# Attention and feed-forward on one core: the first batch's x split from PSUM, and the mask of 14 heads added by TensorE

## The chip, the core and the metric

The kernel runs on one core of one Trainium2 chip. The metric is the device time of one execution in microseconds: 943.42 us before, the median of three runs (942.66 to 944.47). A core has TensorE (PE, matmuls out of SBUF into PSUM), VectorE (DVE), ScalarE (ACT), GpSimd (POOL) and SyncE (SP), which here issues every DMA. Each engine works through its own instructions in order; they meet at semaphores.

## The reference, cut to what matters

Eight batches of eight heads; 512 local and 32 global tokens each; heads of 64. Then a feed-forward layer on all 8 x 544 = 4352 tokens of 512 features.

```python
s_g = scale * q_g @ k_all.T                  # global queries see all 544 keys
out_g = sm(s_g) @ v_all
s_ll = where(|i - j| <= 32, scale * q_l @ k_l.T, -1e9)
s_l = concat([scale * q_l @ k_g.T, s_ll])    # local queries: 32 global keys and a window
out_l = sm(s_l) @ v_all                      # sm: subtract the row's maximum, exp, divide by the sum
x = concat([out_g, out_l]).reshape(4352, 512)
h = x @ w_in                                 # 512 -> 2048
g = h * erf(softplus(h))
out = g @ w_out                              # 2048 -> 512
```

The weights come as 64-bit floats, which the kernel turns into 32-bit ones itself.

## The kernel before, in words

**Precision and matmuls.** Every feed-forward operand is split into a high part, rounded to TensorE's `float32r` type, and a low part, the remainder; a product is three matmuls (high by high, high by low, low by high). `h` of one unit (128 rows of the hidden layer by 512 tokens) is 12 matmuls of 512 columns.

**A pair of heads** (`attention`, line 369). Local queries are taken in 16 windows of 32; each sees an extent of 128 key columns. `scores` fills two PSUM banks `s` for the two heads with 64 small matmuls. Then, for each head: `mask_max` on VectorE adds the mask out of `cs` to each of four blocks of 128 x 128, writes the result to SBUF (`sm`) and takes the row's maximum (`mx`) with the same custom instruction, four per head; a subtraction of the maximum, on VectorE or GpSimd; one exponential on ScalarE over all 512 columns; four transposes on TensorE into a PSUM bank `t`; a copy to `pt`; 16 matmuls with the values (`o`, whose last column is the row's sum); the division (`rs`, `norm`) into `xn`, 128 tokens by 128 features in four blocks.

**From attention to the feed-forward part.** After each second head VectorE transposes `xn` in blocks of 32 x 32 into `xT` (line 474), and four DMAs store it to the DRAM scratch `xsc[b]`, feature rows by tokens, with the tokens of each row in a moved order. Later `load_x` (line 706) loads a batch's x back in two halves, `rx`, and splits each into `xh` (VectorE or ScalarE) and `xl` (GpSimd or VectorE), putting the tokens in order again. `attention_global` (line 502) treats the 32 global queries of four heads at a time; for the first batch it is put off until head 12.

**Two passes over the feed-forward part.** The hidden layer is worked in two halves. The first pass takes one batch after another: `load_x`, eight units of `h` (`unit`), the nonlinearity in groups of four units (`gate`: on ScalarE a table load, four softplus, a table load, four erf, a table load back to the exponential), and the projection `op` (`project`), whose partial result goes to DRAM. The second pass takes batches in pairs with a Strassen-like scheme (`pair_blocks`, `products`: matmuls `pa` to `pd`), and reads `xsc` again, that of the first batch too. A last unit, `h_g`, serves the global tokens.

**Weights.** `to_fp32` (line 614) loads a raw block (`raw`), takes its bits together on VectorE (three integer instructions and one that clears denormals, tile `top`), with one ScalarE instruction beside them; `split` makes the high and low parts. For the first pass four blocks `w_in` and four `w_out` of two halves each are converted during the first heads (keys `WIN`, `WOUT`); `keep_unit` converts the second half of `w_out` to DRAM; `convert_in` the second half of `w_in`, once attention is over.

**What sets the order.** Nothing is ordered by hand. `Program.add` (line 107) takes each operation with its estimated duration on each engine that may run it, a key (a due time in units of the feed-forward part) and the buffers that it reads and writes. `schedule` (line 144) replays the estimates in time: on each free engine it takes the ready operation with the smallest key, no further ahead of the oldest one left than `AHEAD`, if its buffers are free; an operation that two engines could do goes to the one that the estimates favour (`BIAS`). The result is the fixed order of instructions on each engine, SP's DMA queue included. So keys and estimates, not only the operations, decide what the chip runs next. Heads get keys by `HKEYS`: a list of head numbers and keys with straight lines between. While the estimated time is under `FILL` = 50, `filler` puts matmuls on constants (`spare`) where TensorE would be idle, so that its clock stays up.

**PSUM.** Eight banks: two for `h` (pool `h`), six for all else (pool `a`): scores, transposes, values, global attention, projections.

Of the kernel before, what the change touches and what calls it, by code (L numbers as in the profile page):

```python
# [11 lines left out]
F32 = mybir.dt.float32  # L12
# [37 lines left out]
LATER, GFIRST = 12, (-2.0, -1.7)  # L50
NORMAL = 1.125 * 2.0**-15
STRAIGHT = False
# [208 lines left out]
def kernel(  # L261
# [74 lines left out]
    load(HKEYS[0][1] - QLEAD + 0.001, CS, cst, 360)  # L336
    PG = fixed(attn.tile([P, NENT * WB], F32, name="pg"))
# [30 lines left out]

    def attention(b, h, key):
# [15 lines left out]

        if h % 2 == 0:
            st["s"] = SS = [psum_a([P, 4, P], f"s_{nm}_{i}") for i in range(2)]

            def scores():
                for t in range(4):  # L390
                    for i in range(2):
                        for a in range(4):
# [6 lines left out]
                                start=True,  # L399
                                stop=True,  # L400
                            )

            add({"PE": 1.24}, key, scores, [Q, K], SS, heat=2048)
# [4 lines left out]
        def mask_max():  # L408
            for t in range(4):
# [11 lines left out]
        add({"DVE": 0.9}, key, mask_max, [S, CS], [SM, MX])  # L421
        add({"DVE": 0.6, "POOL": 1.03},
            key,
            lambda e: vec[e].tensor_tensor(
                SM.ap, SM.ap, MX.ap.unsqueeze(2).to_broadcast([P, 4, P]), ALU.subtract
            ),
            [MX],
            [SM],
        )
        add({"ACT": 0.62}, key, lambda: act(SM.ap, SM.ap, AF.Exp, scale=scale), [TAB], [SM])  # L430
# [8 lines left out]
        add({"ACT": 0.6, "DVE": 0.6}, key + STEP * 2, lambda e: copy(e, PT.ap, T.ap), [T], [PT])  # L439
# [32 lines left out]
        add({"DVE": 0.335, "ACT": 1.28}, key + STEP * 3, norm, [O, RS], [XN])  # L472
        if h % 2 == 1:
            XT = abuf([P, 4, P], f"xT_{nm}", "xT", 1)
            add({"DVE": 0.62},
                key + STEP * 4,
                lambda: dve.transpose(
                    XT.ap.rearrange("p j (t d) -> p j t d", d=WB), XN.ap.rearrange("p t (j d) -> p j t d", d=WB)
                ),
                [XN],  # L480
                [XT],
            )
            rows = xsc[b][P * p : P * p + P, :].rearrange("(j d) (a x) -> a d j x", d=WB, a=4)

            def store():
                for a in range(4):
                    dma(rows[a], XT.ap[WB * a : WB * a + WB])

            add({"SP": 4 * SPT}, key + STEP * 4, store, [XT, ATTN], [XSC[b, p]], moved=262.0)
# [10 lines left out]
    held, NH, GTURN = [], H, fixed(None)  # L500

    def attention_global(b, j, VA, qk, key):
# [36 lines left out]
        add({"ACT": 0.98}, key, exps, [GA, GB, NM, TAB], [PG])  # L539
# [7 lines left out]
        for T, m0 in ((T1, 0), (T2, 3)):  # L547
            add({"PE": 0.33}, key + STEP * 2, lambda T=T, m0=m0: transposes(T, m0), [PG, CS], [T], heat=384)
            add(
                {"ACT": 0.5, "DVE": 0.46},  # L550
# [41 lines left out]
        add({"DVE": 0.22, "ACT": 0.62}, key + STEP * 3, spread, [O, HALF], [XG])  # L592
# [21 lines left out]
    def to_fp32(key, src, name, TOP, ABS, deps, lead=RLEAD):  # L614
# [7 lines left out]
        add({"ACT": 0.7}, key, lambda: act(ABS.ap(), word(1).bitcast(F32), AF.Abs), [RAW], [ABS.buf])  # L622
# [13 lines left out]
        add({"DVE": 1.55}, key, bits, [RAW], [TOP.buf])  # L636
        add({"DVE": 0.6}, key, normal, [ABS.buf], [TOP.buf])

    def split(key, TOP, HI, LO):
# [625 lines left out]
```

## Time and profile before

| | |
|---|---|
| median of three runs | 943.42 us |
| the profiled execution | 945.86 us |
| its span, first to last instruction | 944.1 us |
| busy: TensorE | 914.6 us (97%) |
| busy: VectorE | 643.0 us (68%) |
| busy: ScalarE | 536.0 us (57%) |
| busy: GpSimd | 401.8 us (43%) |
| DMA traffic | 173.26 MB, mean 184 GB/s |

Times in the profile are microseconds from the span's start unless marked ns. A row of a group reads: line, engine, operation, output<-inputs, shapes, count | busy us, mean ns of one | idle time of the engine just before, and what ended it. Nearly all instructions are recorded under a helper's line (L299 matmuls, L300 transposes, L301 ScalarE, L311 VectorE and GpSimd, L303 DMAs), so they are told apart by their tiles. A row of the timeline begins with its start and its length. Matmuls overlap in the pipeline: a record of 0.39 us can stand for a step of 0.23. SPq is the DMA queue's issuing.

### The profile page before, as it was taken

The numbers are of one execution on the slowest core, as the hardware profiler recorded it, in microseconds if no ns is written. First come the engines' busy times: TensorE is split into PE (matmuls) and PEld (weight loads), VectorE is DVE, ScalarE is ACT, GpSimd is POOL, SyncE is SP. The second block draws the span as 40 slices with busy tenths as digits, with TensorE's granted clock in tenths as the row PEclk, the third lists the DMA queues.
The fourth block names the chain that finished last, engine by engine and source line by source line (L and its number), as shares of the span: only waits on it lengthen the run. The fifth ranks groups of instructions, "written<-read, shape, count | busy, mean of one in ns | idle before, by whom it ended". The sixth has DMA issues, their size and how long they took to land.

```text
span 944.1 us, 22303 instructions
## 1 busy us (share of the span) xinstructions
PE 914.6 (97%) x8937; PEld 736.0 (78%) x8937; DVE 643.0 (68%) x1484; ACT 536.0 (57%) x895; POOL 401.8 (43%) x295
## 2 busy tenths in 40 slices
PE   8899889999999999999999999999999999999997
PEld 6667667777777877777888887888888888888886
DVE  5899799877788685674676959357656446544363
ACT  3547757535586565445766676527727544842590
POOL 1233456332353332132364668334737537541250
PEclk9999899999999999999999999999999999999999
DMA  9876776468677765542406063844642636253422
GB/s 347 278 238 213 231 230 225 138 208 284 209 247 227 238 200 161 163 142 58 157 33 257 34 257 112 310 192 178 234 155 91 239 110 226 81 193 134 157 90 67
DMA packets 89535, 173.26 MB, mean 184 GB/s; under 512 B 13272, under 2 KB 38872, under 8 KB 89432
## 3 DMA queue, kind: packets, MB, share of 16 engines
q1 hardware_dynamic: 89432, 171.84, 54.0%
q8 instruction: 70, 1.15, 0.5%
q14 instruction: 33, 0.27, 0.1%
HBM read 133.53 MB, written 38.27 MB: 182 GB/s over the span
## 4 chain that ended last, share of the span: by engine, by line
PE 79%; DVE 9%; issue 2%; DMA 1%; SPq 0%; ACT 0%; DVEq 0%
PE op L299 37%; PE h L299 16%; PE pc L299 4%; PE pd L299 4%; PE pa L299 4%; DVE top_out L311 3%; PE o L299 2%; PE s L299 2%; PE pb L299 2%; PE t L300 2%; PE h_g L299 1%; PE go L299 1%; PE ga L299 1%; DVE sm L311 1%; PE gt L300 1%
## 5 line engine op out<-in xcount | busy, mean ns | idle before, releaser
L299 PE MATMUL op<-wouth,gh 128*128 128x512 f32 x544 | 218.3, 401 | 0.0
L299 PE MATMUL op<-woutl,gh 128*128 128x512 f32 x544 | 213.2, 392 | 1.2 <-DVE woutl L311 1.2
L299 PE MATMUL op<-wouth,gl 128*128 128x512 f32 x544 | 213.0, 392 | 0.0
L311 POOL TENSOR_TENSOR gl<-sp,gh 128x512 fp32r<-128x512 f32 x66 | 92.7, 1409 | 111.7 <-ACT gh L301 70.0
L299 PEld LDWEIGHTS op<-wouth,gh 128*128 128x128 f32 x544 | 102.7, 189 | 23.3 <-issue 1.4
L299 PEld LDWEIGHTS op<-wouth,gl 128*128 128x128 f32 x544 | 102.7, 189 | 22.1
L302 ACT ACT_TABLE_LOAD x92 | 118.0, 1283 | 2.4 <-PEq L1252 0.7
L299 PEld LDWEIGHTS op<-woutl,gh 128*128 128x128 f32 x544 | 102.9, 189 | 20.9 <-DVE woutl L311 1.5
L301 ACT ACTIVATE gh<-sp 128x512 fp32r<-128x512 f32 x104 | 63.3, 629 | 95.4 <-PE op L299 66.2
L299 PE MATMUL h<-xh,winh 128*128 128x512 f32 (+1 forms) x288 | 113.8, 395 | 0.0
L299 PE MATMUL h<-xh,winl 128*128 128x512 f32 (+1 forms) x288 | 110.2, 383 | 0.0
L299 PE MATMUL h<-xl,winh 128*128 128x512 f32 (+1 forms) x288 | 110.1, 382 | 0.1
L311 POOL TENSOR_TENSOR sm<-sm,mx 128x512 f32<-128x512 f32 x43 | 49.0, 1149 | 131.9 <-DVE mx L311 77.3
L311 DVE TENSOR_TENSOR gl<-sp,gh 128x512 fp32r<-128x512 f32 x70 | 70.7, 1019 | 38.6 <-ACT gh L301 37.3
L311 POOL TENSOR_TENSOR sp<-sp,hs 128x512 f32<-128x512 f32 x46 | 68.3, 1505 | 55.0 <-ACT sp L301 55.0
L301 ACT ACTIVATE sp<-sp 128x512 f32<-128x512 f32 x136 | 75.0, 620 | 0.4
L311 DVE CUSTOM_DVE_ANT_0 sm<-s,cs 128x128 f32<-128x128 f32 x256 | 57.2, 283 | 21.2 <-PE s L299 12.5
L299 PEld LDWEIGHTS h<-xh,winh 128*128 128x128 f32 x288 | 55.0, 191 | 11.3 <-issue 1.4
L299 PEld LDWEIGHTS h<-xh,winl 128*128 128x128 f32 x288 | 54.8, 190 | 10.8
L299 PEld LDWEIGHTS h<-xl,winh 128*128 128x128 f32 x288 | 55.1, 191 | 9.9 <-issue 0.5
L301 ACT ACTIVATE sm<-sm 128x512 f32<-128x512 f32 x64 | 39.9, 631 | 40.5 <-POOL sm L311 35.7
L301 ACT ACTIVATE hs<-h 128x512 f32<-128x512 f32 x44 | 26.2, 595 | 62.0 <-PE h L299 62.0
(186 smaller groups left out, 1824.0 us busy)
## 6 DMA issues: line engine op xcount, KB each, us to landing
wq<-wq SPq DMA_DIRECT2D x28, 896.0 KB, 6.4
vb<-in_vB_dram SPq DMA_DIRECT2D x64, 325.0 KB, 4.0
rx<-xsc SPq DMA_DIRECT2D x32, 512.0 KB, 7.2
va<-in_vA_dram SPq DMA_DIRECT2D x64, 195.0 KB, 3.8
k<-in_kE_dram SPq DMA_DIRECT2D x32, 384.0 KB, 5.7
q<-in_qT_dram SPq DMA_DIRECT2D x32, 272.0 KB, 5.3
part<-os SPq DMA_DIRECT2D x34, 256.0 KB, 3.8
os<-part SPq DMA_DIRECT2D x34, 256.0 KB, 4.1
```

Source lines behind the costliest of these rows:

```text
L299: pe = lambda n, *a, **k: pinned(nc.tensor.matmul(n, *a, **k))
L300: tr = lambda *a, **k: pinned(nc.tensor.transpose(*a, **k))
L301: act = lambda *a, **k: pinned(nc.scalar.activation(*a, **k))
L302: table = lambda name: pinned(nc.scalar.preload_act_table_set(name))
L311: return lambda *a, **k: pinned(f(*a, **k))
```

## The change

It has four parts.

1. **`straight`.** For the first batch, each pair's `xn` is transposed by TensorE (four transposes into a PSUM bank `x`), one copy on ScalarE or VectorE rounds it into the high part, and VectorE subtracts that from the bank into the low part. `load_x(0, 0)` hands these tiles to the units and loads nothing. Since the second pass still wants `xsc[0]`, a third instruction copies the bank to `xT` with the tokens in the moved order, and one DMA stores it, both keyed 1.547 later.
2. **14 front heads** (`FRONT`). `csr` is a `float32r` copy of the mask and the identity. For the first seven pairs, one matmul of 512 columns (identity by mask) starts each score bank, and the 64 small matmuls add onto it. VectorE takes the maxima of all four blocks with one `tensor_reduce` out of PSUM and scales them by -1/8; ScalarE takes the exponential out of PSUM in four instructions with the maxima as bias, and no subtraction is left. The other 50 heads are as before.
3. **Keys.** `HKEYS`, `WIN`, `WOUT`, `KEEP`, `GATE1`, `PROJ1` and most other timing constants have new values.
4. **Estimates.** The durations that the planner assumes are changed in some 25 places (a ScalarE copy of 512 columns 0.58 to 0.52, say); the operations in those places are the same.

```diff
-HKEYS = ((0, -6.35), (8, -3.85), (22, 0.53), (64, 42.58))
-STEP, GKEY = 0.06, -0.15
-QLEAD, VLEAD, RLEAD, XLEAD = 0.755, 0.15, 0.011, 2.0
-GOFF, POFF = 1.27, 4.29
-WIN, WOUT = (-4.26, -3.26, -2.26, -1.26), (4.0, 5.0, 6.0, 7.0)
-KEEP, KSTEP, FIRST = 20.0, 2.5, (6.0, 9.0)
-CV0, CVS, CVO = (46.5, 54.5), 1.8, (71.0, 72.0, 73.0, 74.0)
-QLEAD2, XDEL = 4.0, 1.6
-GATE1, GATE2, PROJ1, PROJ2 = (11.0, 17.0), (20.0, 25.0), 15.0, 23.0
+HKEYS = ((0, -6.695), (8, -5.399), (22, 0.494), (64, 36.876))
+STEP, GKEY = 0.15, -0.654
+QLEAD, VLEAD, RLEAD, XLEAD = 1.111, -0.093, 0.011, 2.475
+GOFF, POFF = 0.46, 5.993
+WIN, WOUT = (-5.592, -4.592, -4.119, -2.592), (0.525, 1.379, 2.986, 3.986)
+FRONT = 14
+KEEP, KSTEP, FIRST = 15.253, 2.161, (8.718, 8.308)
+CV0, CVS, CVO = (44.889, 46.213), 1.64, (73.778, 71.216, 73.428, 75.096)
+QLEAD2, XDEL = 2.637, 2.359
+GATE1, GATE2, PROJ1, PROJ2 = (17.232, 16.792), (19.085, 26.545), 19.111, 19.37
-BIAS, AHEAD = 0.65, 10.4
+BIAS, AHEAD = 0.637, 14.185
-LATER, GFIRST = 12, (-2.0, -1.7)
+LATER, GFIRST = 12, (-3.159, -2.767)
-STRAIGHT = False
+STRAIGHT, XLATE = True, 1.547
...
+    csr = attn.tile([P, 512 + P], F32R, name="csr")
+    add({"ACT": 0.75}, HKEYS[0][1] - 0.01, lambda: copy("ACT", csr, cs[:, : 512 + P]), [CS], [CSR])
...
             def scores():
+                for S in SS if front else ():
+                    pe(S.ap.rearrange("p t k -> p (t k)"), csr[:, 512:], csr[:, :512], start=True, stop=True)
...
-                                start=True,
+                                start=not front,
...
-            add({"PE": 1.24}, key, scores, [Q, K], SS, heat=2048)
+            add({"PE": 1.24 + 0.5 * front}, key, scores, [Q, K, *[CSR] * front], SS, heat=2048)
...
+        def largest():
+            dve.tensor_reduce(MX.ap, S.ap, axis=AX.X, op=ALU.max)
+            dve.tensor_scalar(MX.ap, MX.ap, -scale, None, op0=ALU.mult)
+
+        def exps():
+            for t in range(4):
+                act(SM.ap[:, t, :], S.ap[:, t, :], AF.Exp, bias=MX.ap[:, t : t + 1], scale=scale)
+
+        if front:
+            add({"DVE": 0.8}, key, largest, [S], [MX])
+            add({"ACT": 1.05}, key, exps, [TAB, S, MX], [SM])
+        else:
...
+            if b == 0 and STRAIGHT:
+                straight(p, XN, key)
+            else:
...
+    def straight(p, XN, key):
+        i, j = divmod(p, 2)
+        if j == 0:
+            X0[i] = [mbuf([P, 2, SL], F32R, f"x{x}_0_0_{i}", f"x{x}", 3) for x in "hl"]
+        HI, LO = X0[i]
+        X = psum_a([P, SL], f"x_{p}")
+        def transposes():
+            for t in range(4):
+                tr(X.ap[:, P * t : P * t + P], XN.ap[:, t, :], ident)
+        add({"PE": 0.47}, key + STEP * 4, transposes, [XN, CS], [X], heat=512)
+        add({"ACT": 0.52, "DVE": 0.62}, key + STEP * 4, lambda e: copy(e, HI.ap[:, j, :], X.ap), [X], [HI])
+        add({"DVE": 0.62}, key + STEP * 4,
+            lambda: dve.tensor_tensor(LO.ap[:, j, :], X.ap, HI.ap[:, j, :].bitcast(F32), ALU.subtract), [X, HI], [LO])
...
+        add({"ACT": 0.55, "DVE": 0.69}, key + STEP * 4 + XLATE,
+            lambda e: copy(e, XT.ap.rearrange("p (a t q) -> p t a q", a=4, q=WB), moved(X.ap)), [X], [XT])
+        add({"SP": SPT}, key + STEP * 4 + XLATE, lambda: dma(xsc[0][P * p : P * p + P, :], XT.ap), [XT, ATTN], [XSC[0, p]], moved=262.0)
...
+        if c == 0 and STRAIGHT:
+            return [(*X0[i], j) for i in range(2) for j in range(2)]
```

More of the change, by code (lines that the diff above doesn't have):

```diff
@@ L438, in attention @@
         add({"PE": 0.47}, key + STEP * 2, transposes, [SM, CS], [T, PT], heat=512)
-        add({"ACT": 0.6, "DVE": 0.6}, key + STEP * 2, lambda e: copy(e, PT.ap, T.ap), [T], [PT])
+        add({"ACT": 0.52, "DVE": 0.61}, key + STEP * 2, lambda e: copy(e, PT.ap, T.ap), [T], [PT])
         O = psum_a([P, 4, D + 1], f"o_{nm}")
@@ L470, in norm, with store @@
                     act(XN.ap[:, t, r0 : r0 + D], O.ap[:, t, :D], AF.Copy, scale=RS.ap[:, t, :])
-        add({"DVE": 0.335, "ACT": 1.28}, key + STEP * 3, norm, [O, RS], [XN])
+        add({"DVE": 0.34, "ACT": 0.85}, key + STEP * 3, norm, [O, RS], [XN])
         if h % 2 == 1:
[L474 to L489, printed above, removed]
+            if b == 0 and STRAIGHT:
+                straight(p, XN, key)
+            else:
+                XT = abuf([P, 4, P], f"xT_{nm}", "xT", 1)
+                add({"DVE": 0.62},
+                    key + STEP * 4,
+                    lambda: dve.transpose(
+                        XT.ap.rearrange("p j (t d) -> p j t d", d=WB), XN.ap.rearrange("p t (j d) -> p j t d", d=WB)
+                    ),
+                    [XN],
+                    [XT],
+                )
+                rows = xsc[b][P * p : P * p + P, :].rearrange("(j d) (a x) -> a d j x", d=WB, a=4)
+                def store():
+                    for a in range(4):
+                        dma(rows[a], XT.ap[WB * a : WB * a + WB])
+                add({"SP": 4 * SPT}, key + STEP * 4, store, [XT, ATTN], [XSC[b, p]], moved=262.0)
         if h % 4 == 3:
@@ L549, in attention_global @@
             add(
-                {"ACT": 0.5, "DVE": 0.46},
+                {"ACT": 0.42, "DVE": 0.48},
                 key + STEP * 2,
@@ L760, in unit @@
         Hb = mbuf([P, SL], F32, f"hs_{nm}", "hs", 7)
-        add({"ACT": 0.58, "DVE": 0.69}, key, lambda e: copy(e, Hb.ap, HP.ap.rearrange("p a t -> p (a t)")), [HP], [Hb])
+        add({"ACT": 0.52, "DVE": 0.62}, key, lambda e: copy(e, Hb.ap, HP.ap.rearrange("p a t -> p (a t)")), [HP], [Hb])
         return v, Hb, ()
@@ L797, in gate @@
             )
-            add({"DVE": 0.43, "ACT": 0.62}, k, lambda e, SPb=SPb, GH=GH: copy(e, GH.ap, SPb.ap), [SPb, *after], [GH, *turn])
+            add({"DVE": 0.43, "ACT": 0.55}, k, lambda e, SPb=SPb, GH=GH: copy(e, GH.ap, SPb.ap), [SPb, *after], [GH, *turn])
             add(
@@ L846, in project @@
             if ps == 0:
-                add({"ACT": 0.58, "DVE": 0.69}, k, lambda e, t=t, O=O: copy(e, O.ap, OP[t].ap), [OP[t]], [O])
+                add({"ACT": 0.52, "DVE": 0.62}, k, lambda e, t=t, O=O: copy(e, O.ap, OP[t].ap), [OP[t]], [O])
                 add({"SP": SPT},
@@ L916, in part_of @@
                 add(
-                    {"POOL": 0.72, "DVE": 0.4},
+                    {"POOL": 0.88, "DVE": 0.4},
                     k,
@@ L1004, in lo @@
                     )
[L1006 removed]
+            add({"DVE": 0.95, "ACT": 1.1}, k, hi, [A], [HI])
             add({"POOL": 2.8, "DVE": 1.55}, k, lo, [A, HI], [LO])
@@ L1069, in move @@
         def move(out, n, k):
-            add({"ACT": 0.58, "DVE": 0.69}, k, lambda e: copy(e, out.ap, bank[n].ap), [bank[n]], [out])
+            add({"ACT": 0.52, "DVE": 0.62}, k, lambda e: copy(e, out.ap, bank[n].ap), [bank[n]], [out])
         k = [key + 4 * i / 7 for i in range(7)]
@@ L1099, in block @@
             HI, LO = (Buf(pool, [P, 2, n], F32R, f"g{x}_{name}", tag) for x, (pool, tag) in zip("hl", XTAG[2 * m : 2 * m + 2]))
-            add({"DVE": 0.5, "ACT": 0.62}, k, lambda e: copy(e, HI.ap, A.ap), [A], [HI])
+            add({"DVE": 0.5, "ACT": 0.55}, k, lambda e: copy(e, HI.ap, A.ap), [A], [HI])
             add(
@@ L1136, in last_unit @@
         Hb = mbuf([P, SL], F32, f"hs_g{q}", "hs", 7)
-        add({"ACT": 0.58, "DVE": 0.69}, key, lambda e: copy(e, Hb.ap, HP.ap.rearrange("p a t -> p (a t)")), [HP], [Hb])
+        add({"ACT": 0.52, "DVE": 0.62}, key, lambda e: copy(e, Hb.ap, HP.ap.rearrange("p a t -> p (a t)")), [HP], [Hb])
         return q, Hb, ()
```

61 lines of the change are left out of this document (40 added, 21 removed).

## The prediction

> **What bounds the kernel now.** I read the page's head first, then the table of busy time by stage, the groups of the first 60 us, the timelines of VectorE, ScalarE and the DMA queue around the first batch, and last the waits of TensorE.
>
> ```profile
> span 944.1 us, 22303 instructions
> 0.00:40.00 40.00, 34.63 (x820) 26.77 (x824) 24.44 (x124) 14.04 (x23) 7.56 (x11) 1.00 0.88 308
> 40.00:80.00 40.00, 37.59 (x746) 28.10 (x746) 38.36 (x120) 23.04 (x53) 12.84 (x10) 1.00 0.85 278
> 80.00:120.00 40.00, 34.00 (x638) 26.04 (x617) 34.29 (x122) 29.74 (x51) 21.82 (x17) 0.87 0.63 196
> 120.00:160.00 40.00, 37.05 (x574) 28.19 (x573) 38.05 (x98) 25.33 (x49) 22.65 (x17) 0.96 0.80 258
> 160.00:300.00 140.00, 134.91 (x1990) 105.65 (x1989) 114.37 (x350) 78.83 (x144) 56.23 (x42) 0.99 0.67 213
> 500.00:900.00 400.00, 398.01 (x1843) 332.23 (x1842) 234.45 (x294) 224.59 (x343) 200.98 (x137) 1.00 0.47 170
> ```
>
> The columns after the stage and its length are busy us of TensorE, its weight loads, VectorE, ScalarE and GpSimd, then TensorE's granted clock, the DMA share and GB/s. From 500 to 900 us TensorE is busy 398.0 of 400: there the time is matmul work, and nothing that the change does to the first batch shortens it. From 40 to 160 us VectorE is busy 38.4 + 34.3 + 38.1 = 110.7 of 120. That is the engine that sets the pace while weights are converted and heads computed. In the first 40 us VectorE is busy only 24.4, and the DMA engines are at 0.88: there the inputs' arrival counts.
>
> ```profile
> L299 PE MATMUL spare<-const-bfloat16-1.0 128*128 128x256 bf16 x169 | 25.2, 294 | 0.8 <-PEq L1252 0.8
> 60.93 0.48 PE L299 MATMUL h<-xh,winh 128*128 128x512 f32 x1
> ```
>
> TensorE looks busy early, but 25.2 us of its first 60 are filler matmuls into `spare`. The first useful matmul of the feed-forward part, `h`, starts at 60.93. In 0 to 160 us TensorE's idle time is 5.4 + 2.4 + 6.0 + 3.0 = 16.7 us; with the filler there are about 42 us of room. That is the ceiling for the change. A microsecond that VectorE saves before 160 us is worth a microsecond at the end, since the matmuls behind simply move forward; nothing saved after that is.
>
> **The first batch's x.** Before, it goes through DRAM:
>
> ```profile
> 26.40 7.59 SPq L303 DMA_DIRECT2D xsc<-xT  x12
> 38.64 0.70 DVE L311 STREAM_TRANSPOSE xT<-xn 128x512 f32<-128x512 f32 x1
> 46.89 0.38 SPq L303 DMA_DIRECT2D rx<-xsc  x1
> 55.56 1.16 ACT L301 ACTIVATE xh<-rx 128x512 fp32r<-128x512 f32 x2
> 56.28 2.50 POOL L311 TENSOR_TENSOR xl<-rx,xh 128x512 fp32r<-128x512 f32 x2 [2.07 <-ACT xh L301]
> ```
>
> The last pair of heads is transposed at 38.64; the low half of its x is written at 56.28 + 2.50 = 58.78, and `h` follows at 60.93. So 20.1 us lie between the last attention result of batch 0 and a usable x. After the change the path is four PE transposes, one copy and one subtraction. For those:
>
> ```profile
> 60.30 0.66 PE L300 MATMUL t<-cs,sm 128*128 128x128 f32 x4
> L301 ACT ACTIVATE pt<-t 128x512 f32<-128x512 f32 x39 | 22.6, 594 | 28.7 <-PE t L300 28.6
> L311 DVE TENSOR_TENSOR os<-op,os 128x512 f32<-128x512 f32 x34 | 23.3, 689 | 20.0 <-PE op L299 18.4 <-DMA wq<-wq 1.3
> ```
>
> 0.66 + 0.60 + 0.69 = 2.0 us, so x stands ready about 18 us sooner. On VectorE the change removes four stream transposes, 4 x 0.70 = 2.8 us; it adds four subtractions, 4 x 0.69 = 2.8, and eight copies (HI and the store's XT) that ScalarE (0.59) or VectorE (no more than the 0.69 of a subtraction) may take. Bounds for VectorE's share of these are 0 and 8 x 0.69 = 5.5 us; I take the middle, 2.8, because the planner gives both engines nearly the same price. XT is no longer read by the first pass; it is read again late, by the second, so its copy and its store have hundreds of microseconds. On the DMA queue 16 stores become 4 and two loads of x go: twelve stores took 7.59 us, 0.63 each, so about 12 x 0.63 = 7.6 us of the queue come free, and in the row above those twelve stand ahead of value and weight loads.
>
> GpSimd loses the subtraction of the first x, and with it a hidden cost on VectorE:
>
> ```profile
> 45.76 2.69 POOL L311 TENSOR_TENSOR xl<-rx,xh 128x512 fp32r<-128x512 f32 x2 [4.38 <-ACT xh L301]
> 43.63 1.42 DVE L311 SCALAR_TENSOR_TENSOR top_in<-raw_in,top_in 128x512 int32<-128x512 int32 x2
> 47.36 2.36 DVE L311 SCALAR_TENSOR_TENSOR top_in<-raw_in,top_in 128x512 int32<-128x512 int32 x2
> 57.50 1.31 DVE L311 TENSOR_SCALAR gh<-cs,gr 128x2 f32<-128x2 f32 x1
> 83.00 0.23 DVE L311 TENSOR_SCALAR gh<-cs,gr 128x2 f32<-128x2 f32 x1
> ```
>
> The same two VectorE instructions take 1.42 us alone and 2.36 beside GpSimd's subtraction of x at 45.76, and a tiny one takes 1.31 instead of 0.23 beside the other at 56.28. That is 0.9 + 1.1 = 2.0 us, which goes with the two pairs of `xl`.
>
> **The 14 heads.** Exactly 14 heads lie in the first 60 us (56 instructions, four a head):
>
> ```profile
> L311 DVE CUSTOM_DVE_ANT_0 sm<-s,cs 128x128 f32<-128x128 f32 x56 | 12.5, 285 | 14.8 <-PE s L299 7.5 <-PE t L300 7.3
> L311 DVE TENSOR_TENSOR sm<-sm,mx 128x512 f32<-128x512 f32 x7 | 5.5, 781 | 0.1
> 7.50 0.29 DVE L311 CUSTOM_DVE_ANT_0 sm<-s,cs 128x128 f32<-128x128 f32 x1 [7.50 <-PE s L299]
> 9.31 0.79 DVE L311 TENSOR_TENSOR sm<-sm,mx 128x512 f32<-128x512 f32 x1
> 40.08 0.66 DVE L311 TENSOR_REDUCE gm<-ga 128x1 f32<-128x480 f32 x1
> 40.65 0.28 DVE L311 CUSTOM_DVE_ANT_0 sm<-s,cs 128x128 f32<-128x128 f32 x1
> L311 DVE TENSOR_SCALAR rs<-o 128x4 f32<-128x4 f32 x12 | 1.7, 151 | 0.0
> ```
>
> Two heads' masks and maxima run from 7.50 to 9.31, 0.905 us a head. Seven of the 14 subtractions are VectorE's. Before: 14 x 0.905 + 5.5 = 18.2 us. After: one reduction of 512 elements out of PSUM (480 elements: the next instruction starts 0.57 later; scaled, 0.61; its full 0.66, scaled, 0.70) and a scaling of four numbers, 0.15. That is 0.76 to 0.85 a head, 10.6 to 11.9 us. VectorE saves 6.3 to 7.6; I take 7. Little of it falls where VectorE is the bound:
>
> ```profile
> 0.00:40.00 40.00, 13.05 (x48) 1.00 0.88 308
> ```
>
> Of VectorE's writes of `sm`, 48 lie before 40 us: four subtractions and 44 maxima, eleven heads. Only three heads come later; their part is 3/14 of 7.0, 1.5 us. The seven subtractions on GpSimd lay beside other work, so I count nothing for them.
>
> On ScalarE one exponential becomes four with a bias of their own:
>
> ```profile
> L301 ACT ACTIVATE sm<-sm 128x512 f32<-128x512 f32 x14 | 8.7, 632 | 13.8 <-POOL sm L311 13.4 <-DVE sm L311 0.4
> 43.68 0.93 ACT L301 ACTIVATE xn<-o,rs 128x64 f32<-128x64 f32 x4
> L301 ACT ACTIVATE pg<-ga,gn 128x480 f32<-128x480 f32 x16 | 10.6, 659 | 6.2 <-DVE gn L311 6.0
> L301 ACT ACTIVATE pg<-gb,gn 128x64 f32<-128x64 f32 x16 | 5.0, 310 | 0.0
> ```
>
> From 64 to 480 elements an exponential with a bias grows by (659 - 310) / 416 = 0.84 ns an element, so four of 128 take about 0.93 + 4 x 0.054 = 1.15 us in a row, against 0.63: 14 x 0.52 = 7.3 us more on ScalarE. It is busy 14.0 of 40 and 23.0 of 40 us in those stages, and no head waits for a subtraction any more, so I count nothing; if the cover were gone it would cost those 7.3. The Trainium skill (ScalarE: Activation LUTs, What ACT_TABLE_LOAD costs) speaks against this edit: a per-partition bias adds about 93 ns to each activation and neighbours overlap by as much; by its figures four would be estimated at 1.27 us, and the addition at 14 x 0.64 = 9 us. No instruction of just this shape is in the trace before, so the rows' 7.3 stays in the sum's cover.
>
> On TensorE each of seven pairs gets two matmuls of 512 columns, and four pairs get four transposes.
>
> ```profile
> 107.84 2.73 PE h L299 x12
> ```
>
> At 2.73 / 12 = 0.23 us, 14 mask matmuls are 3.2 us and the transposes 4 x 0.66 = 2.6; 5.8 us together, hidden by the 25.2 us of filler. Without that cover they would cost 5.8.
>
> **The sum.** In the stretch that VectorE bounds: -1.5 (heads) and -2.0 (GpSimd's interference), -3.5 us. Ahead of 40 us VectorE's empty time is 15.6 us, and becomes 15.6 + 5.5 (the other heads) - 2.8 (copies of x) = 18.3. What can fill it is conversion work, if its data is there: the queue has 7.6 us less to issue, and the first `w_in` is keyed ahead of the eighth head (from -4.26 to -5.59). Nothing of it filled and 12 us (two thirds) are the bounds; I take 5.7, below the middle, since the DMA engines are at 0.88 already. Together -9.2 us. The profiled execution took 945.86 (span 944.1 and 1.8 around it), which gives 936.7; the median of the three runs is 2.4 lower, so I predict 934 us. The retimed keys of the later stages and the repriced planner costs I set at zero: 160 to 300 us has 5.1 us of idle TensorE, so from -4 to, by symmetry, +4. The terms' bounds alone give -3.5 to -15.5, or 928 to 940.
>
> **The rivals.** *Deeper.* x is ready 18 us sooner, so `h` could start near 43 us and take the filler's place; the empty spots at 80 to 160 us would also close. For it speaks the clock:
>
> ```profile
> PE s L299 <- DVE top_out L311: 3.5, 1, 3.5
> 102.50 0.63 PE L299 MATMUL h<-xh,winl 128*128 128x512 f32 x1
> 105.16 0.39 PE L299 MATMUL h<-xh,winh 128*128 128x512 f32 x1
> ```
>
> After TensorE had waited 3.5 us for VectorE's conversion of `w_out`, its matmuls took 0.63 us for a while, then 0.39 again. At the granted 0.87 and 0.96 the two stages lose 34.0 x 0.13 + 37.1 x 0.04 = 5.9 us. With that, and 10 us of the early hole filled, it is -3.5 - 10 - 5.9 = -19.4, so 924. Against it: eight conversions of `w_in` still queue on VectorE whatever x does. The Trainium skill (TensorE: Matmul & The Clock Gate, HAM oscillation — how this bites in real kernels) says that an idle gap over some 3.4 us drops the clock to half; the 3.5 us wait agrees with it, and a shorter wait would then keep all of it. Chance 0.18.
>
> *Swallowed.* Nothing of the early hole is filled: the next thing late is `w_in`, whose loads still come after the heads' inputs on full DMA engines, so early x only waits. Then the -3.5 us of the bound stretch are all, and if VectorE makes its copies of x after 40 us, -0.7: 940 to 942.7. Chance 0.14, half of it inside what counts as no change.
>
> *Slower.* The score banks are now released by ScalarE's exponentials, not by VectorE's maxima.
>
> ```profile
> 80.54 1.28 ACT L302 ACT_TABLE_LOAD   x1
> 87.55 1.28 ACT L302 ACT_TABLE_LOAD   x1
> ```
>
> A gate of four units holds ScalarE from 80.54 to 88.83, 8.3 us, for nothing else. If x and `h` come so early that gates stand ahead of the last front pairs' exponentials, two of the six PSUM banks of pool `a` stay taken, the next scores wait behind them on TensorE, and VectorE gets no maxima. One gate takes back 8.3 of the 9.2; two make it +7.4, near 951 by the median. It decides as soon as a second gate passes a front pair. Against it: all 14 exponentials were done by 60 us, 20 us before the first gate. With a partial second block it starts above 945. Chance 0.16. That x isn't really freed from DRAM I exclude: the first pass takes HI and LO straight from the split.
>
> **How the numbers follow.** Forecast 0.52, deeper 0.18, swallowed 0.14, slower 0.16. The measurement tells about 0.2%, 1.9 us, from no change. Faster: 0.52 + 0.18 + 0.05 of swallowed = 0.75; no change 0.09; slower 0.16. The range 923 to 947 takes in the deeper case and the beginning of the slower one and leaves out under 2 in 10.
>
> **What would show it.** The first `h` between 43 and 52 us; VectorE's maxima as 14 reductions near 0.7 us and four ScalarE exponentials near 0.36 us each; GpSimd without `sm` in the first heads; four `xsc` stores for batch 0; less than 34 us of VectorE in one of the stages from 40 to 160; the stage after 300 us as before but earlier. Wrong would be: the first `h` later than 56, ScalarE as releaser of scores in TensorE's waits for several microseconds, a granted clock under 0.9 for longer than before, or a gain that sits after 500 us.

## The result and the profile after

The kernel became slower: 952.85 us, the median of 6 runs (950.65 to 958.35), against 944.33 for the kernel before beside it (942.66 to 947.43). The ratio is 1.0101, interval [1.0079, 1.0122]. The profiled execution took 952.05, span 950.0. The forecast was 934.0 with a range of 923 to 947.

First the span and the table of busy time by stage, as for the kernel before: TensorE, weight loads, VectorE, ScalarE, GpSimd, then granted clock, DMA share and GB/s.

```profile
span 950.0 us, 22213 instructions
0.00:40.00 40.00, 36.55 (x756) 27.86 (x757) 20.54 (x58) 18.79 (x54) 0.94 (x5) 0.96 0.78 285
40.00:80.00 40.00, 37.80 (x747) 28.11 (x746) 34.92 (x93) 28.67 (x73) 8.69 (x7) 1.00 0.84 271
80.00:120.00 40.00, 32.72 (x646) 24.21 (x644) 39.08 (x111) 30.96 (x58) 27.17 (x19) 1.00 0.73 230
120.00:160.00 40.00, 38.72 (x543) 30.34 (x544) 36.16 (x102) 25.37 (x45) 21.16 (x15) 0.96 0.68 228
160.00:300.00 140.00, 131.08 (x2046) 100.47 (x2045) 122.17 (x363) 88.76 (x168) 62.71 (x47) 1.00 0.71 226
500.00:900.00 400.00, 396.24 (x1820) 330.03 (x1820) 270.36 (x313) 217.24 (x330) 189.73 (x119) 1.00 0.46 164
```

VectorE from 40 to 160 us is busy 110.2, as before (110.7). Before 40 us it is empty for 19.5 us (15.6 before), so the early hole wasn't filled at all. Some 2 us of it are new at its start: the first maxima begin at 9.88 us (7.50 before, 7.86 in e12, which has the new early keys without the new heads), behind the copy `csr` and the mask matmuls. The sum had left that out. TensorE idles 8.9 us from 160 to 300 (5.1 before) and 3.8 from 500 to 900 (2.0 before).

The heads do what was costed. The groups of the first 60 us on TensorE, VectorE and ScalarE:

```profile
L300 PE MATMUL spare<-const-bfloat16-1.0 128*128 128x256 bf16 x126 | 20.5, 307 | 0.8 <-PEq L1311 0.8
...
L312 DVE TENSOR_REDUCE mx<-s 128x4 f32<-128x512 f32 x14 | 9.6, 683 | 11.6 <-PE s L300 10.8 <-ACT sm L302 0.5
L312 DVE TENSOR_SCALAR mx<-mx 128x4 f32<-128x4 f32 x14 | 2.4, 170 | 0.5
...
L302 ACT ACTIVATE sm<-s,mx 128x128 f32<-128x128 f32 x56 | 15.6, 386 | 5.7 <-DVE mx L312 5.7
```

VectorE's two new steps take 9.6 + 2.4 = 12.0 us for 14 heads; 10.6 to 11.9 were forecast. The score banks are not held back by ScalarE: nobody waits long for `sm`.

Now x, as the timelines of VectorE, the DMA queue and TensorE show it:

```profile
26.73 7.67 SPq L304 DMA_DIRECT2D xsc<-xT  x2
39.75 0.91 SPq L304 DMA_DIRECT2D raw_in<-in_w_in_dram  x2
44.07 0.69 DVE L312 TENSOR_TENSOR xl<-x,xh 128x512 fp32r<-128x512 f32 x1
54.19 0.68 DVE L312 TENSOR_TENSOR winl<-top_in,winh 128x512 fp32r<-128x512 f32 x1
55.21 0.48 PE L300 MATMUL h<-xh,winh 128*128 128x512 f32 x1
```

x is whole at 44.76, 14.0 us sooner than before (58.78). But the first `h` starts at 55.21, only 5.7 sooner. It starts 0.3 us after the low part of `w_in` is there (54.19 + 0.68), and that weight's load was issued at 39.75. Ahead of it on the queue two stores of x stood for 7.67 us. In the kernel before, twelve stores had stood there for 7.59. So the length of that row is not the price of issuing twelve stores: here it ends when the copy `xT` that the second store reads is done, at 34.0 us.

Late in the kernel two things are new. At the passage into the second pass TensorE waits once, for 3.62 us, and then runs slowly. Its timeline after, and the same passage before, where it waits three times for 2.0 us in all:

```profile
584.97 0.50 PE L300 MATMUL pc<-xh_B,wq_c 128*128 128x512 f32 x1 [3.62 <-DVE pair L312]
586.14 0.63 PE L300 MATMUL pc<-xl_B,wq_c 128*128 128x512 f32 x1
```

```profile
580.95 0.51 PE L299 MATMUL pd<-xl_T,wq_c 128*128 128x512 f32 x1 [0.73 <-DVE xl_T L311]
...
585.48 0.50 PE L299 MATMUL pa<-xh_B,wq_c 128*128 128x512 f32 x1 [1.05 <-DVE c L311]
...
588.71 0.50 PE L299 MATMUL pc<-xh_B,wq_c 128*128 128x512 f32 x1 [0.20 <-DVE pair L311]
```

And at the very end, VectorE's last addition, before and after:

```profile
939.36 0.69 DVE L311 TENSOR_TENSOR os<-op,os 128x512 f32<-128x512 f32 x1 [0.67 <-PE op L299]
```

```profile
942.42 0.69 DVE L312 TENSOR_TENSOR os<-op,os 128x512 f32<-128x512 f32 x1 [0.67 <-PE op L300]
```

From its start to the end of the span it takes 944.1 - 939.36 = 4.7 us before, and 950.0 - 942.42 = 7.6 after. In the order of the DMA queue the last store was `os_7_3`, 128 rows in one piece; now it is `os_8_1`, four pieces of 32 rows.

### The profile page after: what moved, and what is told of

Same layout as the page of the kernel before. It is cut to its first block, busy times and chain, and to the rows that moved or that the text cites. A ratio compares the mean times of both kernels' runs of the same rounds, so it can differ in the third digit from the quotient of the medians.

```text
span 950.0 us, 22213 instructions
## 1 busy us (share of the span) xinstructions
PE 914.4 (96%) x8924; PEld 734.9 (77%) x8924; DVE 683.0 (72%) x1422; ACT 536.4 (56%) x921; POOL 389.6 (41%) x273
## 3 DMA queue, kind: packets, MB, share of 16 engines
q8 instruction: 70, 1.15, 0.5%
## 4 chain that ended last, share of the span: by engine, by line
PE 81%; DVE 11%; issue 2%; DMA 2%; POOL 1%; ACT 1%; SPq 0%; DVEq 0%; ACTq 0%
PE op L300 35%; PE h L300 16%; PE pd L300 4%; PE pc L300 4%; PE pa L300 4%; PE s L300 3%; PE o L300 3%; PE t L301 3%; DVE top_out L312 2%; PE pb L300 2%; PE spare L300 2%; DVE gl L312 1%; DVE top_in L312 1%; DMA raw_in<-in_w_in_dram 1%; PE h_g L300 1%
## 5 line engine op out<-in xcount | busy, mean ns | idle before, releaser
L312 POOL TENSOR_TENSOR gl<-sp,gh 128x512 fp32r<-128x512 f32 x52 | 77.6, 1495 | 106.0 <-PE op L300 51.3
L302 ACT ACTIVATE gh<-sp 128x512 fp32r<-128x512 f32 x89 | 54.9, 628 | 105.2 <-PE op L300 86.9
L312 DVE TENSOR_TENSOR gl<-sp,gh 128x512 fp32r<-128x512 f32 x84 | 94.6, 1130 | 19.3 <-ACT gh L302 10.9
L312 POOL TENSOR_TENSOR sm<-sm,mx 128x512 f32<-128x512 f32 x32 | 35.3, 1107 | 95.3 <-DVE mx L312 51.5
L312 DVE TENSOR_TENSOR os<-op,os 128x512 f32<-128x512 f32 x34 | 23.3, 690 | 43.8 <-PE op L300 43.0
L312 DVE CAST gh<-sp 128x512 fp32r<-128x512 f32 x47 | 28.6, 611 | 35.0 <-PE op L300 35.0
```

What stands on the lines that cost most here:

```text
L302: act = lambda *a, **k: pinned(nc.scalar.activation(*a, **k))
L312: return lambda *a, **k: pinned(f(*a, **k))
```

## The experiments

The runs separate three things that the change does at once: the two parts (x, heads), the early keys with the planner's prices, and the late keys. Ratios are to the kernel before, run on the same chip; the kernel before lay at 944.9 to 945.5.

**e1, both parts with the old keys and prices.** All constants of the kernel before, `STRAIGHT = True`, `FRONT = 14`.

> The two parts (x split from PSUM, 14 front heads) with every key and every planner price of the kernel before. Theory K (the parts help, the new keys and prices lose more than they bring): 3 to 10 us faster than before, first h before 55 us. Theory P (the parts themselves cost, through banks held longer or more ScalarE work): slower than before by 4 us or more. Theory S (any change reshuffles the planner's greedy order, and the time moves by some us either way): within 5 us of before, with the difference spread over stages that the parts do not touch.

961.51 us, 1.0180 [1.0120, 1.0240]. So the parts alone, on the old keys, don't help.

**e2, new keys and prices, neither part.** `STRAIGHT = False`, `FRONT = 0`, no `csr`.

> The keys and prices of the changed kernel, but neither part (no front heads, first x through DRAM). Theory K: 6 us or more slower than before, at least as slow as the changed kernel (952 and up). Theory P: like before, 942 to 946. Theory S: anywhere from 942 to 956, with losses at other places than in the changed kernel.

954.71 us, 1.0099 [1.0071, 1.0127]: the whole loss without either part.

**e3, a control**: `(22, 0.53)` to `(22, 0.55)` in the kernel before.

> The kernel before with one key of no importance moved (heads' key at head 22 from 0.53 to 0.55). A control: no operation is added or changed. Theories K and P: within 1 us of before. Theory S: 3 us or more away from before, in either direction, which would mean that a single pair of kernels cannot price a part.

945.67 us, 0.9996 [0.9974, 1.0019]. But in the trace every engine has the same order as in the kernel before: the nudge moved nothing. So the run is a repeat. It shows that the same order gives the same time; whether any other order would cost as much (theory S) it can't say.

**e4, x's store later.**

```diff
-        add({"SP": SPT}, key + STEP * 4 + XLATE, lambda: dma(xsc[0][P * p : P * p + P, :], XT.ap), ...
+        add({"SP": SPT}, key + STEP * 4 + XLATE + 4.0, lambda: dma(xsc[0][P * p : P * p + P, :], XT.ap), ...
```

> The changed kernel with the four stores of the first batch's x keyed 4 units later (the copies to XT stay). In the changed kernel's trace the DMA queue stands for 7.7 us at 26.7 us on two of these stores, and the second w_in block is issued only at 39.8. If that head-of-line wait is what keeps w_in and so h late: first h 5 us or more earlier than 55 us, time 3 to 7 us shorter than the changed kernel's 952. If the wait is covered (theory K or P alone): within 1.5 us of the changed kernel.

954.33 us, 1.0093 [1.0064, 1.0122], but the edit did not do what it was for. The planner takes what is ready when the queue is free, whatever its key within `AHEAD`; the two stores still went out at 26.74 and stood for 8.02 us. In the trace every engine has the order of the changed kernel, so this too is a repeat. It says nothing about the queue; e9 mends it.

**e5, late keys old.** The changed kernel with

```diff
-KEEP, KSTEP, FIRST = 15.253, 2.161, (8.718, 8.308)
-CV0, CVS, CVO = (44.889, 46.213), 1.64, (73.778, 71.216, 73.428, 75.096)
-QLEAD2, XDEL = 2.637, 2.359
-GATE1, GATE2, PROJ1, PROJ2 = (17.232, 16.792), (19.085, 26.545), 19.111, 19.37
+KEEP, KSTEP, FIRST = 15.253, 2.161, (6.0, 9.0)
+CV0, CVS, CVO = (46.5, 54.5), 1.8, (71.0, 72.0, 73.0, 74.0)
+QLEAD2, XDEL = 4.0, 1.6
+GATE1, GATE2, PROJ1, PROJ2 = (11.0, 17.0), (20.0, 25.0), 19.111, 23.0
...
-    key = s + 4 + POFF
+    key = s + 4 + 4.29
```

(the last line for the last block only; `PROJ1` and `POFF` elsewhere stay). TensorE's order is the same up to matmul row 2924, about 500 us.

> The changed kernel with the keys of its last stages taken back to those of the kernel before: conversions of the second pass's weights (CV0, CVS, CVO), QLEAD2, XDEL, FIRST, GATE1, GATE2, PROJ2 and the key of the last block's projection (4.29 for POFF). The planner then writes the same TensorE order up to matmul row 2924 (near 500 us), so both parts, all early keys and all prices stay. Theory L (the late keys cost, at the passage into the second pass near 585 us and in the last store): the 3.6 us wait of pc on pair and the matmuls at 0.63 us after it go (3 to 5 us), the drain after the last addition falls from 7.6 to about 4.7 us (2.85): 945 to 947 us, beside 952.9 for the changed kernel. Theory E (the loss lies in the early stages and in the work that the prices send to VectorE): 951 to 954, the wait at 585 turning up in another place.

945.85 us, 1.0011 [0.9989, 1.0032]. The loss is gone. The wait at the passage is 1.92 us for 3.62, and from the last addition to the end of the span it is 945.8 - 942.11 = 3.7 us for 7.6. Theory L holds. The forecast gain isn't there either: with the late keys taken back, the change is worth nothing that can be told.

**e6, the tail alone.** The changed kernel with only `PROJ2` 23.0 and `key = s + 4 + 4.29`.

> The changed kernel with only two late keys taken back: PROJ2 19.37 to 23.0 and the last block's projection to 4.29 for POFF. The order is the same up to matmul row 3890; at the end the store of os_8_1 (four pieces of 32 rows) no longer stands last, four stores of os_7 do. Theory L: start of the last addition to end of span 4.7 us for 7.6, time 2.9 us less: 950. Rival: the drain is bound by the last matmul and the last store alike, whichever it is: no change, 952 to 954.

949.15 us, 1.0033 [1.0008, 1.0058]. The last addition:

```profile
943.69 0.69 DVE L312 TENSOR_TENSOR os<-op,os 128x512 f32<-128x512 f32 x1 [0.67 <-PE op L300]
```

The span ends at 947.3, 3.6 us later. So 4.0 us of the tail came back. By the ratios the run is 0.68% faster than the changed kernel, 6.4 us, with an uncertainty of 3; by the medians, taken on two chips, 3.7. Either way it is over half of what the late keys cost. The rival, that the drain is the same whichever store is last, falls.

**e7 and e8, one part at a time on all new keys** (`FRONT = 0` with no `csr`; `STRAIGHT = False`).

> New keys and prices, only the part that splits x out of PSUM (FRONT = 0, no rounded mask). Beside 954.7 with neither part and 952.9 with both. If the early x is what helps: first h at about 55 us and 951 to 953. If the heads are what helps: 954 to 956. If stalls of TensorE on its own instruction stream decide (16 us in all with neither part, 8 with both): anywhere from 949 to 960, and the sum of these stalls follows the time.

> New keys and prices, only the 14 heads with mask matmul and single reduction; x goes through DRAM. If the early x is what helps: first h at 62 to 64 us and 954 to 956. If the heads are what helps: 951 to 953. If stalls of TensorE on its instruction stream decide: the time follows their sum, anywhere from 949 to 960.

x alone: 963.01 us, 1.0180 [1.0129, 1.0231] (954.4 to 964.5). Heads alone: 951.46 us, 1.0065 [1.0040, 1.0091]. The heads help against e2, the early x costs. The sum of the stalls does not follow the time: 5.6 us with x alone, the least of the four, in its fastest run.

**e9, x's store behind `w_in`.** e5, and the store's operation also reads `*W["in", 0, 1]`, which only the planner sees.

> e5 (both parts, late keys of the kernel before; 945.9) with the four stores of the first batch's xT ordered behind the conversion of w_in's second unit, in the planner's order only, so that they no longer stand on the DMA queue ahead of value, query and w_in loads. Theory W (the early x is swallowed because two stores wait 7.7 us at the queue's head for the copies and the loads of w_in stand behind them): the loads of raw_in that were issued at 39.8 us go out some 5 to 7 us earlier, first h at 48 to 51 us instead of about 55, and 940 to 943. Rival C (VectorE and ScalarE, or the transfers themselves, set the conversions): the loads go out earlier, but h moves by less than 2 us and the time stays at 944 to 947.

944.48 us, 0.9983 [0.9960, 1.0006]; first `h` at 54.85. The stores now go out after 56 us, and the loads of `raw_in` still wait. From the DMA queue's timeline and its waits from 18 to 58 us:

```profile
23.04 3.41 SPq L304 DMA_DIRECT2D va<-in_vA_dram  x5
36.81 0.33 SPq L304 DMA_DIRECT2D vb<-in_vB_dram  x1
...
39.94 0.90 SPq L304 DMA_DIRECT2D raw_in<-in_w_in_dram  x2
```

```profile
SPq L304 <- PE o L300: 10.2, 2, 9.5
```

In the store's place the next load, `vb`, waits 9.5 us for a buffer that the heads' values (`o`) still read. The stores were not the only thing at the queue's head: behind one wait stood another, which ended at about the same time.

**e10, each mask matmul twice.** e5 with `for S in [*SS, *SS] if front else ():`.

> e5 with each of the 14 mask matmuls issued twice (the second overwrites the first): 14 matmuls of 512 columns more on TensorE in the first 60 us, 14 x 0.23 = 3.2 us, everything else in the same order. Theory H (the prediction's: filler and waits cover TensorE's added work there): no change, 945 to 947. Theory T (TensorE's added work is on the path, as the filler is a fixed part of its order and each early us is matmul work, filler or a wait on it): 948 to 950.

946.70 us, 1.0015 [0.9997, 1.0033], against 1.0011 for e5. The groups of TensorE's first 60 us, of e5 and of e10:

```profile
L300 PE MATMUL s<-csr 128*128 128x512 f32 x14 | 5.0, 438 | 0.0
```

```profile
L300 PE MATMUL s<-csr 128*128 128x512 f32 x28 | 8.4, 420 | 0.1
```

3.4 us more of busy time cost nothing that can be told: 0.04%, 0.4 us, with an uncertainty of 2.6. That speaks for theory H: the added matmuls lie under TensorE's waits.

**e11, fetches shifted.** e1 with this ahead of everything:

```diff
+    for _ in range(32):
+        pe(spare[:, :16], warm[:, :P], warm[:, :16], start=True, stop=True)
```

> e1 (both parts on the old keys; 961.5, of which 17.6 us in the profile are waits of TensorE on nothing that the profile shows) with 32 matmuls of 16 columns (64 instructions with their weight loads) put ahead of everything on TensorE, where it waits for the first inputs. Theory F (these waits are TensorE's instruction fetches, one every 256 of its instructions, long where the DMA engines are full): the waits move to other matmuls, 64 instructions earlier in the stream, and their sum changes by several us, with the time following it: 950 to 960 if it falls to about 8. Rival (the waits belong to the work at those places, not to the count of instructions): the waits stay at the same matmuls, sum 16 to 19, time 960 to 963.

956.69 us, 1.0110 [1.0072, 1.0149], against 1.0180: 0.7% less, with an uncertainty as large. TensorE's timeline in e1 at its longest stalls, and the DMA share during the first of them:

```profile
141.85 0.86 PE L300 MATMUL go<-va,gt 128*32 128x65 f32 x44
146.66 0.31 PE L300 MATMUL go<-va,gt 128*32 128x65 f32 x4 [3.95 <-issue]
...
214.85 0.85 PE L300 MATMUL go<-va,gt 128*32 128x65 f32 x42
218.85 0.44 PE L300 MATMUL go<-va,gt 128*32 128x65 f32 x6 [3.15 <-issue]
```

```profile
142.70:146.60 3.90, 0.01 (x1) 0.00 (x0) 0.67 (x5) 3.87 (x7) 1.21 (x1) 1.00 1.03 373
```

The same two groups of 48 `go` in e11:

```profile
140.88 0.43 PE L300 MATMUL go<-va,gt 128*32 128x65 f32 x11
144.02 0.77 PE L300 MATMUL go<-va,gt 128*32 128x65 f32 x36 [2.71 <-issue]
...
213.11 0.39 PE L300 MATMUL go<-va,gt 128*32 128x65 f32 x10
215.82 0.77 PE L300 MATMUL go<-va,gt 128*32 128x65 f32 x38 [2.32 <-issue]
```

In e1 the stalls come after 44 and 42 of the 48 matmuls, in e11 after 12 (one more lies among rows not shown) and 10: 32 earlier both times, exactly the 32 put in. So the stall belongs to a place in the count of TensorE's instructions, not to the work, as a fetch of instructions would; the last section shows the transfers. All such waits sum to 17.6 us in e1, 12.3 in e11 and 6.9 before.

**e12, early keys and prices alone, late keys old** (e5 with neither part).

> e2 (new keys and prices, neither part; 954.7) with the late keys taken back as in e5. With e5 it shows what both parts do when the late stages are the old ones. If the late keys cost the same here as in e5 (7 us): 947 to 948, and the parts are worth 1 to 2 us. If the parts bring what the prediction said, 9 us: 955, which would mean that the late keys cost nothing without the parts. If the early keys alone are already as good as the parts: 945 to 946.

950.72 us, 1.0044 [1.0014, 1.0074]: the early keys and prices cost some 4 us without the parts. Both parts together (e5) bring 0.33% of it back, 3 us by the ratios and 5 by the medians, with an uncertainty of 3.5.

**e13 and e14, `w_in` first.** e9 with `WIN[0]` -6.4; and with -6.6 and -5.9 for the first two.

> e9 with one key changed: the first unit of w_in from -5.592 to -6.4, so that its second half and the second unit's first half stand on the DMA queue ahead of the value loads that waited there for the heads' buffers (until 36.8 us in e9). Theory Q (the queue's order holds w_in back, and the store at its head was only the first of two waits in a row): raw_in goes out near 26 to 31 us instead of 39.9, first h at 45 to 48 us instead of 54.9, and 937 to 942. Theory P (TensorE, VectorE and the DMA engines have the same work before 160 us whenever h begins: an earlier h only delays the heads that come after): first h earlier by the same 7 to 9 us, and the time within 943 to 946.

> As e13, with the first unit of w_in at -6.6 and the second at -5.9, so that the third and fourth loads too come ahead of the value loads of the next heads. Theory Q: first h at 45 to 48 us, the second unit's first h some us earlier too, 936 to 942. Theory P: 943 to 947, since the heads of the second batch begin later by what h begins earlier.

e13: 944.61 us, 0.9991 [0.9975, 1.0007]. e14: 958.42 us, 1.0146 [1.0100, 1.0191]. The timelines of e13:

```profile
27.54 0.84 SPq L304 DMA_DIRECT2D raw_in<-in_w_in_dram  x2
...
46.19 0.66 DVE L312 TENSOR_TENSOR winl<-top_in,winh 128x512 fp32r<-128x512 f32 x1
47.91 0.68 DVE L312 TENSOR_TENSOR xl<-x,xh 128x512 fp32r<-128x512 f32 x1
...
55.95 0.27 PE L300 MATMUL o<-va,pt 128*32 128x65 f32 x2 [2.35 <-issue]
56.15 0.50 PE L300 MATMUL h<-xh,winh 128*128 128x512 f32 x1
```

The load goes out 12 us sooner, weight and x are both there at 48.6, and yet `h` starts at 56.15: in TensorE's fixed order it stands behind scores, global attention and values of heads, and behind a stall of 2.35 us on the way. Theory Q falls. P holds for e13 in its time, though its earlier `h` did not come; e14, 14 us slower, fits neither.

**e15, e12 with the 32 small matmuls of e11.**

> e12 (early keys and prices alone, no parts, late keys old; 950.7, of which 15.4 us in the profile are TensorE's waits on its instruction stream, against 6.9 before) with the 32 small matmuls of e11 ahead of everything. Theory F (most of what the early keys seem to cost, 5 us, is where the fetches fall): the sum of these waits falls to 7 to 12 and the time to 943 to 948. Rival K (the early keys cost 5 us by their order of the work): 950 to 951 whatever the waits sum up to.

952.37 us, 1.0068 [1.0043, 1.0093]. The waits on instructions sum to 13.6 us, 15.4 before the shift: the fall to 7 to 12 that theory F asked for did not come, nor a gain. As the waits stayed, the run doesn't decide between F and K. What the early keys cost is not shown to be the fetches.

**e16, e17, e18, one part at a time**: heads alone and x alone on e5's keys, heads alone on the old keys.

> e5 without the split of x out of PSUM: the 14 heads alone, new early keys and prices, late keys old. Between neither part (e12, 950.7) and both (e5, 945.9). If the heads bring the 5 us: 945 to 947. If the early x brings them: 950 to 951. If both bring half: 948.

> e5 without the new heads: x split out of PSUM alone, new early keys and prices, late keys old. If the early x brings the 5 us: 945 to 947. If the heads bring them: 950 to 951. With e7 in mind, where x alone came to 963 beside 954.7 with neither, it may also cost: 955 to 959 (late keys 7 lower).

> The kernel before with its own keys and prices (for the heads the prices of their two new steps), and only the 14 new heads. Both parts on these keys took 961.5, 16 us more than before, 10 of them in waits on the instruction stream. If the prediction's account of the heads holds on the order it was made for (1.5 us saved in the stretch that VectorE bounds, TensorE's mask matmuls covered): 942 to 944. If any change on the old keys upsets the order and the fetches: 950 to 962.

e16: 943.60 us, 0.9985 [0.9969, 1.0000]. e17: 957.44 us, 1.0134 [1.0116, 1.0152]. e18: 959.01 us, 1.0142 [1.0124, 1.0160]. On the new early keys the heads bring the gain and x costs; on the old keys the heads cost. In e17 TensorE's longest wait is new:

```profile
PE go L300 <- ACT pg L302: 7.2, 1, 7.2
```

It ends at 120.28. The chain of waits leads from `pg` back through the maxima `gm` to VectorE's conversions of `w_out` (`top_out`, from 112.84 to 118.88). VectorE is busy 9.93 of the 10 us from 110 to 120, and two of its instructions take more than twice as long there, beside GpSimd's `sp`, as earlier. VectorE's timeline of e17, then GpSimd's:

```profile
101.86 1.42 DVE L312 SCALAR_TENSOR_TENSOR top_out<-raw_out,top_out 128x512 int32<-128x512 int32 x2
113.89 3.31 DVE L312 SCALAR_TENSOR_TENSOR top_out<-raw_out,top_out 128x512 int32<-128x512 int32 x2
113.53 3.13 POOL L312 TENSOR_TENSOR sp<-sp,hs 128x512 f32<-128x512 f32 x2
```

What x costs shows in this stage. From 80 to 120 us TensorE idles longer with x than without it in all four pairs on the new keys: 11.7 us to 4.1 (e17, e12), 8.1 to 3.7 (e5, e16), 11.8 to 4.7 (e7, e2), 7.3 to 3.4 (after, e8).

All runs of the parts and keys in one table, as change against the kernel before:

| keys and prices | neither part | x alone | heads alone | both |
|---|---|---|---|---|
| old | 0 | | +1.42% (e18) | +1.80% (e1) |
| new early, old late | +0.44% (e12) | +1.34% (e17) | -0.15% (e16) | +0.11% (e5) |
| all new | +0.99% (e2) | +1.80% (e7) | +0.65% (e8) | +1.01% (after) |

Read along the second row and down the last column, the change is a sum of four: early keys and prices +0.44%, heads -0.59%, x +0.26%, late keys +0.90%: 1.01% in all. Each carries an uncertainty of some 0.3%, so x's +0.26% alone can't be told from nothing, and each depends on the path: in the four pairs on new early keys the heads are worth 0.34 to 1.23%. For x and the late keys the sign holds on every path: x is dearer with than without it in all five pairs of the table (+0.26 to +0.90), and the late keys in all four columns (+0.46 to +0.90).

e16 is the best version found; against the kernel before it is at the edge of what can be told, against the changed kernel 1.2% faster.

## Why the prediction was wrong

**The step that failed** is one sentence: "The retimed keys of the later stages and the repriced planner costs I set at zero". Its bounds, -4 to +4, were argued from TensorE's idle time from 160 to 300 us. The late keys alone cost 0.90%, 8.5 us with an uncertainty of 3 (e5), and none of it lies there: TensorE idles 8.6 us from 160 to 300 in e5 and 8.9 in the changed kernel. 4.0 us are the last store (e6), and part of the rest is the passage near 585 us, where the wait is 1.7 us longer than in e5. The early keys and prices cost another 0.44% (e12); they do lose in that stage, where e12 idles 9.3 us and the kernel before 5.1. Of the stretch after 500 us the prediction had said that "nothing that the change does to the first batch shortens it"; that is so, but the keys could lengthen it.

**"x stands ready about 18 us sooner"**: 14.0 us, so nearly. But it brought no time. In e13 weight and x were both there at 48.6 and the end did not move. The second step that failed is therefore the reason given in "is worth a microsecond at the end, since the matmuls behind simply move forward". First `h` and ratio in eight runs (the kernel before: 60.9):

| | e11 | e1 | e5 | e9 | after | e13 | e16 | e12 |
|---|---|---|---|---|---|---|---|---|
| first `h`, us | 49.6 | 51.9 | 53.8 | 54.9 | 55.2 | 56.2 | 64.1 | 64.8 |
| ratio | 1.0110 | 1.0180 | 1.0011 | 0.9983 | 1.0101 | 0.9991 | 0.9985 | 1.0044 |

The earliest `h` belongs to two of the longest times, and the three shortest have it anywhere from 54.9 to 64.1. In a fixed order on each engine `h` stands behind what was put ahead of it (e13), and with x early TensorE waits more from 80 to 120 us instead.

**The early hole, -5.7**: nothing. VectorE is empty for 19.5 us of the first 40; the conversions' data was not there, and TensorE's order wouldn't have used them earlier (e13). One premise was misread: "about 12 x 0.63 = 7.6 us of the queue come free". That row was mostly waiting, and two stores waited just as long, 7.67 us. This is the rival *swallowed*, which had been given 0.14, in its mechanism though not in its time. The 2.0 us of GpSimd's interference came back in the main: the conversion that took 2.36 us beside `xl` takes 1.44 (at 47.01), the tiny `gh` 0.86 instead of 1.31 (at 52.56, now beside GpSimd's `winl`). Yet in 40 to 160 us VectorE is as busy as it was, other work having moved in.

**The heads**: right in their parts. 12.0 us for VectorE; ScalarE's four exponentials hidden; TensorE's mask matmuls hidden (e10). Their worth, 0.59% or 5.6 us with x still in DRAM (uncertainty 3 us), is near the 7 us saved on VectorE and more than the 1.5 that the sum let count. On the old keys the same heads cost 1.42%.

The Trainium skill (ScalarE: Activation LUTs, What ACT_TABLE_LOAD costs) had led to an estimate of 1.27 us for the four exponentials of a head. Here four alone take 1.12 to 1.18 us, as the 1.15 from the rows said, and eight in a row, two heads, take 2.17:

```profile
17.70 2.17 ACT L302 ACTIVATE sm<-s,mx 128x128 f32<-128x128 f32 x8
```

That is 1.08 a head. Both lie below the estimate.

***Slower*, 0.16**, named nearly the right time, 951, by a mechanism that did not occur: the front pairs' exponentials are over before the first gate at 77.9 us, and nobody waits for their banks. That the time came out near is luck. *Deeper* did not occur; the clock from 80 to 120 us is at 1.00 instead of 0.87, as it asked, but TensorE idles 7.3 us there instead of 6.0, and the clock of the first 40 us fell from 1.00 to 0.96.

Of the signs named, the first `h` came at 55.2, outside the 43 to 52 asked for; the reductions (0.68), the single exponentials (0.39) and the DMA queue's four stores of batch 0 came as said; VectorE's 34 us was not undercut in any stage.

What stays open is why the early keys and prices cost 0.44% and why heads on the old keys cost 1.42%. Longer waits on TensorE's instructions go along with both (15.4 us in e12 and 12.2 in e18, for 6.9 before), but the shift in e15 did not remove them, and e17 is 1.3% slower with 10.4. The granted clock goes along too: the mean over the runs is 0.984 to 0.988 in e1, e7, e14, e17 and e18, all 1.3% or more slower, and 0.992 to 0.993 in the kernel before. No run separates the waits from the clock. Theory S isn't excluded as a part of it, since e3 left the order as it was: on top of e9, e13 moved one key and came to 0.9991, e14 moved two and came to 1.0146. So a term of the table is the worth of an edit in the order that the planner made of it.

## What to carry to other kernels

Where a planner fixes the order, constants that are retuned along with an edit are an edit of their own: undo them stage by stage, and look first at the passage between stages and at the last store, where this kernel lost most of what the late keys cost. Make sure, before a run is called a control, that the planner's order did change. Before counting a result that is ready sooner, follow what its consumer waits for next, and then what stands ahead of that consumer on its engine. Judge a new step on more than one set of keys: the same heads were worth -0.6% on the new early keys and +1.4% on the old ones.

## What the runs showed of the hardware

Three things were not expected.

TensorE stops for 1 to 4 us at fixed places in its own instruction count. The profile calls it a wait for "issue". It moves with the count and not with the work, 32 matmuls for 32 put in. The trace shows what it waits for: in the 20 profiles 45 such waits last 1.7 us or more, and during every one of them a transfer of 16 KB runs on a queue that the profile calls "instruction"; TensorE goes on 1.2 to 1.6 us after its end. In e1 the transfer runs from 144.44 to 145.39 us and the matmuls go on at 146.66. The row of that queue on the page of e1, and in the 3.9 us of the first stall:

```profile
q8 instruction: 70, 1.15, 0.5%
```

```profile
q8 instruction: 1, 0.02, 1.5%
```

Most of the 70 transfers stop nothing. What makes some of them late is not shown: the DMA share was 0.87 to 1.05 during the six long stalls of e1, but 0.67 during one of the kernel before.

The drain goes with the shape of the last store: 7.6 us when four pieces of 32 rows stood last, 3.6 to 4.7 when 128 rows in one piece did. In the last stretch of the changed kernel, 944 to 948 us, the DMA share is 0.20 to 0.26, three to four of the 16 engines; in the kernel before it is 0.82 and 0.74 in the two us from 940 to 942.

After the wait at the passage TensorE's granted clock can fall to 0.50 for 3.4 us; matmuls then take 0.63 us instead of 0.39. In the changed kernel the wait was 3.62 us, but in e5 a wait of 1.92 us had the same effect, and in e4, whose order is that of the changed kernel, 3.62 us had none. e5, then e4:

```profile
583.39 0.50 PE L300 MATMUL pc<-xh_B,wq_c 128*128 128x512 f32 x1 [1.92 <-DVE pair L312]
...
584.57 0.63 PE L300 MATMUL pc<-xl_B,wq_c 128*128 128x512 f32 x1
```

```profile
588.35 0.50 PE L300 MATMUL pc<-xh_B,wq_c 128*128 128x512 f32 x1 [3.62 <-DVE pair L312]
588.69 0.39 PE L300 MATMUL pc<-xl_B,wq_c 128*128 128x512 f32 x1
```

At this place the clock fell in five of the six profiles with a wait of 3.6 us and in four of the nine with 1.9. So the length alone doesn't decide, and what else does is not shown. The Trainium skill (TensorE: Matmul & The Clock Gate, HAM oscillation — how this bites in real kernels) asks for no idle gap above some 3.4 us; five of the six agree, and the 1.92 us of e5 shows that a shorter one can be enough.
